# A linear-attention and channel-mix kernel rewritten: strided token tiles, k side first, normalised q features, token-major second matmul, loads on two queues, and a pipeline ordered by hand

## Chip, cores and metric

One core of one Trainium2 chip. The metric is the time of one execution on the device, in microseconds (us). All kernels named here were run on the chip; those of one experiment round share one chip and are timed beside runs of the kernel before. The changed kernel itself ran in a round of its own, so it and the experiments are compared across chips; the kernel before took a median of 303.0 to 304.1 us in all rounds. Every run has a state, fast or slow (slow: over 1.5% above the fastest run of the same kernel).

PE is the matmul engine, PEld its weight loads, DVE the vector engine, ACT the scalar engine, POOL the GpSimd engine, SP the engine that issues most DMA.

## The reference, cut to what matters

```python
# q, k, v: (4 batches, 4 heads, 1088 tokens, 32); S1, S2: (8, 32)
def phi(x):                                   # 64 features per token and head
    a = S1 x ; b = S2 x                       # 8 each
    return outer(a, b).reshape(64)
kv  = sum_s phi(k_s) v_s^T                    # 64 x 32 per batch and head
z   = sum_s phi(k_s)                          # 64
x   = (phi(q) kv) / (phi(q) . z + 1e-6)       # heads side by side: 128 wide
# then an RWKV channel mix on x (4 x 1088 x 128), d_ff = 1024
xk  = mu_k * x + (1 - mu_k) * x_prev          # x_prev: the token before
xr  = mu_r * x + (1 - mu_r) * x_prev
out = sigmoid(xr w_r) * (relu(xk w_k)**2 w_v)
```

The output is float32, (4, 1088, 128).

## The kernel before

Per batch: 9 tiles of 128 consecutive tokens (the last has 64). Only the parts that the argument touches are shown; cuts are marked.

```python
for b in range(B):
    # ... loads in tiles of 128 tokens: q_sb, k_sb, v_sb, all on the SP queue, runs of 128 bytes
    for t in range(n_tiles):                         # PE transposes of q and k, DVE copies
        nc.tensor.transpose(qtp[:, :m], q_sb[:m, t, :, :]..., ident[:m, :m])
        nc.vector.tensor_copy(qT_sb[:, t, :m], qtp[:, :m])
        # ... the same for k
    for t in range(n_tiles):                         # projections, float32
        nc.tensor.matmul(abk_ps[:], kT_sb[:, t, :], S12T_bd...)
        nc.tensor.matmul(abq_ps[:], qT_sb[:, t, :], S12T_bd...)
        # ... two DVE copies
    # ... k_p, q_p: outer products on DVE, 128 x 2304
    for h in range(H):
        for t in range(n_tiles):                     # L159, L160
            nc.tensor.transpose(qpT_ps[:, :m], q_p[:m, t, h, :], ident[:m, :m])
            nc.vector.tensor_copy(qpT_sb[:, t, :m], qpT_ps[:, :m])
        for t in range(n_tiles):                     # L164
            nc.tensor.matmul(kv_p[:], k_p[:tsz(t), t, h, :], v_sb[:tsz(t), t, h, :], ...)
        # ... kv_cat: 64 x 33, the 33rd column is z
        for t in range(n_tiles):                     # L175
            nc.tensor.matmul(num_ps[:, t, :], qpT_sb[:, t, :], kv_cat[:], ...)
        # ... divide by the 33rd column on DVE
    # ... transposes of x into xT
for b in range(B):                                   # channel mix
    # ... xk_bf, xr_bf on DVE
    while off < S:                                   # 512 tokens at a time
        for c in range(nchunks):                     # 8 chunks of d_ff
            nc.tensor.matmul(kpsum[:, :m], wk[:, c * P:(c + 1) * P], xk_bf[:, off:off + m])
            nc.scalar.activation(krelu[:, :m], kpsum[:, :m], RELU)
            nc.vector.tensor_mul(k2_bf[:, :m], krelu[:, :m], krelu[:, :m])
            nc.tensor.matmul(vvT_p[:, :m], wv[:, c, :], k2_bf[:, :m], ...)
        # ... gate, product, PE transposes back to token-major, stores
```

## Time and profile before

| | before |
|---|---|
| time, median of the first 3 runs | 302.0 us |
| PE, DVE, ACT busy | 259.5, 170.5, 50.3 us |
| attention / channel mix | 0 to about 225 us / 215 to 303 us |
| DMA packets | 62242, mostly under 512 bytes |

The first and second part of the page, before: busy time of each engine, and rows of 40 slices of the span, with the busy share in tenths, the clock granted to PE in tenths, and what DMA moved.

```profile
PE 259.5 (86%) x1212; PEld 184.6 (61%) x1212; DVE 170.5 (56%) x617; ACT 50.3 (17%) x110; POOL 0.7 (0%) x6
PE   0258799999979999998899999959979999698984
PEclk9999999999999999999555555555886559859798
GB/s 70 167 118 92 122 88 117 40 2 51 120 52 2 0 0 0 2 0 0 3 0 0 0 2 0 0 0 2 0 1 2 0 0 59 18 75 0 74 0 77
```

The chain of waits that ended last, before: by engine, and by line of the kernel.

```profile
PE 73%; DVE 12%; SPq 4%; DMA 4%; issue 3%; ACT 2%; DVEq 0%; ACTq 0%
PE num_ps L175 19%; PE qpT_ps L159 14%; PE kv_p L164 12%; PE vvT_p L214 5%; PE abk_ps L138 5%; PE abq_ps L139 5%; PE kpsum L209 5%; DVE k_p L150 3%; PE xtr_ps L187 3%; DVE k_bf L213 2%; PE qtp L125 2%; PE ktp L129 2%; ACT krelu L211 2%; DMA _t_96<-in_moe_w_r_dram 2%; PE otp L230 2%
```

### The profile page before, as it was taken

How to read it: one execution, taken by the hardware profiler on the slowest of the kernel's cores; microseconds unless marked ns; L12 is line 12 of the kernel's file. 1: busy time of each engine (PE TensorE's matmuls, PEld its weight loads, DVE VectorE, ACT ScalarE, POOL GpSimd, SP SyncE). 2: the span in 40 equal slices, each digit the busy share in tenths (PEclk: the TensorE clock that was granted, in tenths of full speed). 3: DMA queues.
4: the chain of work that ended last, by engine and by line, in shares of the span. 5: the costliest groups of instructions: out<-in, count | busy, mean ns of one | idle time of the engine just before them, and what ended most of it. 6: DMA issues, size and time to landing. Idle time of an engine off the chain costs nothing.

```text
span 303.0 us, 3582 instructions
## 1 busy us (share of the span) xinstructions
PE 259.5 (86%) x1212; PEld 184.6 (61%) x1212; DVE 170.5 (56%) x617; ACT 50.3 (17%) x110; POOL 0.7 (0%) x6
## 2 busy tenths in 40 slices
PE   0258799999979999998899999959979999698984
PEld 0127688667968866796677778948555654333432
DVE  3234733554374355448734445693646569877674
ACT  1000000000000000001000000000443146458682
POOL 0000000000000000000000000000000000000000
PEclk9999999999999999999555555555886559859798
DMA  3975757203730000000000000000000002020202
GB/s 70 167 118 92 122 88 117 40 2 51 120 52 2 0 0 0 2 0 0 3 0 0 0 2 0 0 0 2 0 1 2 0 0 59 18 75 0 74 0 77
DMA packets 62242, 10.27 MB, mean 34 GB/s; under 512 B 56592, under 2 KB 62096, under 8 KB 62224
## 3 DMA queue, kind: packets, MB, share of 16 engines
q1 hardware_dynamic: 62224, 10.04, 18.6%
q8 instruction: 10, 0.16, 0.2%
q14 instruction: 8, 0.07, 0.1%
HBM read 7.81 MB, written 2.23 MB: 33 GB/s over the span
## 4 chain that ended last, share of the span: by engine, by line
PE 73%; DVE 12%; SPq 4%; DMA 4%; issue 3%; ACT 2%; DVEq 0%; ACTq 0%
PE num_ps L175 19%; PE qpT_ps L159 14%; PE kv_p L164 12%; PE vvT_p L214 5%; PE abk_ps L138 5%; PE abq_ps L139 5%; PE kpsum L209 5%; DVE k_p L150 3%; PE xtr_ps L187 3%; DVE k_bf L213 2%; PE qtp L125 2%; PE ktp L129 2%; ACT krelu L211 2%; DMA _t_96<-in_moe_w_r_dram 2%; PE otp L230 2%
## 5 line engine op out<-in xcount | busy, mean ns | idle before, releaser
L211 ACT ACTIVATE krelu<-kpsum 128x512 bf16<-128x512 f32 (+1 forms) x96 | 43.0, 471 | 242.7 <-PE kpsum L209 149.6
L175 PE MATMUL num_ps<-kv_cat,qpT_sb 64*128 64x33 f32 x288 | 59.6, 378 | 0.0
L175 PEld LDWEIGHTS num_ps<-kv_cat,qpT_sb 64*128 64x128 f32 x288 | 57.6, 304 | 2.6 <-DVE qpT_sb L160 1.9
L159 PE MATMUL qpT_ps<-ident,q_p 128*64 128x128 f32 x144 | 51.9, 396 | 2.6 <-DVE qpT_sb L160 2.0
L160 DVE COPY qpT_sb<-qpT_ps 64x128 f32<-64x128 f32 x144 | 37.8, 274 | 22.4 <-PE qpT_ps L159 18.8
L164 PE MATMUL kv_p<-v_sb,k_p 128*64 128x33 f32 (+1 forms) x288 | 37.2, 297 | 8.2 <-DVE k_p L150 8.2
L164 PEld LDWEIGHTS kv_p<-v_sb,k_p 128*64 128x64 f32 (+1 forms) x288 | 33.5, 221 | 14.7 <-DVE k_p L150 9.8
L209 PE MATMUL kpsum<-xk_bf,wk 128*128 128x512 bf16 (+1 forms) x96 | 35.1, 386 | 5.3 <-ACT r_sb L220 2.0
L159 PEld LDWEIGHTS qpT_ps<-ident,q_p 128*64 128x64 f32 x144 | 18.8, 133 | 28.4 <-DVE qpT_sb L160 18.5
L214 PE MATMUL vvT_p<-k_bf,wv 128*128 128x512 bf16 (+1 forms) x96 | 32.6, 373 | 3.1 <-DVE k_bf L213 2.6
L213 DVE TENSOR_TENSOR k_bf<-krelu 128x512 bf16<-128x512 bf16 (+1 forms) x96 | 31.3, 339 | 6.7 <-ACT krelu L211 4.0
L125 PE MATMUL qtp<-ident,q_sb 128*128 128x128 f32 (+1 forms) x36 | 15.6, 434 | 17.1 <-DMA q_sb<-in_q_dram 16.0
L177 DVE MEMSET num_ps<- 64x33 f32 x16 | 1.4, 86 | 49.7 <-PE num_ps L175 49.7
L138 PE MATMUL abk_ps<-S12T_bd,kT_sb 128*128 128x64 f32 x72 | 22.5, 416 | 0.7 <-DVE abk_sb L140 0.7
L139 PE MATMUL abq_ps<-S12T_bd,qT_sb 128*128 128x64 f32 x72 | 22.5, 415 | 0.0
L214 PEld LDWEIGHTS <-wv 128*128 128x128 bf16 x96 | 10.9, 115 | 15.2 <-issue 11.9
L125 PEld LDWEIGHTS qtp<-ident,q_sb 128*128 128x128 f32 (+1 forms) x36 | 6.9, 192 | 21.3 <-issue 12.4
L138 PEld LDWEIGHTS abk_ps<-S12T_bd,kT_sb 128*128 128x128 f32 x72 | 18.0, 308 | 3.0 <-DVE abk_sb L140 2.0
L139 PEld LDWEIGHTS abq_ps<-S12T_bd,qT_sb 128*128 128x128 f32 x72 | 17.8, 305 | 1.0 <-DVE abq_sb L141 0.2
L209 PEld LDWEIGHTS <-wk 128*128 128x128 bf16 x96 | 11.0, 116 | 11.1 <-issue 8.5
L129 PE MATMUL ktp<-ident,k_sb 128*128 128x128 f32 (+1 forms) x36 | 15.5, 429 | 1.5 <-DMA k_sb<-in_k_dram 1.0
L127 DVE COPY qT_sb<-qtp 128x128 f32<-128x128 f32 (+1 forms) x36 | 9.8, 274 | 6.6 <-PE qtp L125 6.6
(53 smaller groups left out, 162.8 us busy)
## 6 DMA issues: line engine op xcount, KB each, us to landing
q_sb<-in_q_dram SPq DMA_DIRECT2D x32, 64.0 KB, 2.6
k_sb<-in_k_dram SPq DMA_DIRECT2D x32, 64.0 KB, 2.6
v_sb<-in_v_dram SPq DMA_DIRECT2D x32, 64.0 KB, 2.6
out_dram<-outT_s SPq DMA_DIRECT2D x4, 512.0 KB, 3.4
_t<-in_moe_w_k_dram SPq DMA_DIRECT2D x1, 512.0 KB, 3.3
_t_92<-in_moe_w_v_dram SPq DMA_DIRECT2D x1, 512.0 KB, 5.4
S12T_bd<-in_S_dram SPq DMA_DIRECT2D x8, 1.0 KB, 3.4
q_sb<-in_q_dram SPq DMA_DIRECT2D x4, 32.0 KB, 2.5
```

Source lines behind the costliest of these rows:

```text
L125: nc.tensor.transpose(qtp[:, :m], q_sb[:m, t, :, :].rearrange("p h d -> p (h d)"), ident[:m, :m])
L129: nc.tensor.transpose(ktp[:, :m], k_sb[:m, t, :, :].rearrange("p h d -> p (h d)"), ident[:m, :m])
L138: nc.tensor.matmul(abk_ps[:], kT_sb[:, t, :], S12T_bd[:].rearrange("p h x -> p (h x)"))
L139: nc.tensor.matmul(abq_ps[:], qT_sb[:, t, :], S12T_bd[:].rearrange("p h x -> p (h x)"))
L159: nc.tensor.transpose(qpT_ps[:, :m], q_p[:m, t, h, :], ident[:m, :m])
L160: nc.vector.tensor_copy(qpT_sb[:, t, :m], qpT_ps[:, :m])
L164: nc.tensor.matmul(kv_p[:], k_p[:tsz(t), t, h, :], v_sb[:tsz(t), t, h, :], start=(t == 0), stop=(t == n_tiles - 1))
L175: nc.tensor.matmul(num_ps[:, t, :], qpT_sb[:, t, :], kv_cat[:], start=st, stop=sp)
L209: nc.tensor.matmul(kpsum[:, :m], wk[:, c * P:(c + 1) * P], xk_bf[:, off:off + m])
L211: nc.scalar.activation(krelu[:, :m], kpsum[:, :m], RELU)
L213: nc.vector.tensor_mul(k2_bf[:, :m], krelu[:, :m], krelu[:, :m])
L214: nc.tensor.matmul(vvT_p[:, :m], wv[:, c, :], k2_bf[:, :m], start=(c == 0), stop=(c == nchunks - 1))
```

## The change

Its intent, as the code shows it: token s of a batch is written s = 17 p + t, so that one partition holds 17 consecutive tokens and a load moves runs of 2176 bytes; a tile holds 64 tokens of each of two batches. The sums over k are done first, for a half (two batches) at a time. The normaliser is turned into a projection (SW holds S2-weighted z), and q features are divided before the product with kv, so that x comes out feature-major, as the channel mix needs it. The second channel-mix matmul takes the squares as the stationary operand and gives tokens on the partitions, so that no output is transposed. Small matmuls are split over the array with tile positions. A loop over groups of 4 tiles runs the channel mix of group g beside the attention of groups g+2 and g+3.

The core of the diff, cut:

```diff
-        for t in range(n_tiles):
-            nc.sync.dma_start(q_sb[:m, t, :, :], q[b, :, s0:s0 + m, :].rearrange("h p d -> p h d"))
+    def load_tok(x, src, eng, b2):          # half on the SP queue, half on the GpSimd queue
+        eng.dma_start(tok[x][64 * b2:64 * b2 + 64],
+                      src[2 * int(x[1]) + b2].rearrange("h (s t) d -> s h t d", t=NT))
+    def load_hd(x, src):                    # head-major, for 32x32 transposes on DVE
+        nc.sync.dma_start(hd[x][:], src[...].rearrange("h (a c t) d -> (h a) c t d", a=32, c=2))
...
+    def transp_tok(dst, x, t0, t1):         # L154
+        for t in range(n):
+            for h in range(H):
+                nc.tensor.matmul(tp[D * h:D * h + D, t * P:t * P + P], tok[x][:, h, t0 + t, :], ident[:],
+                                 tile_position=(0, D * h))
+        nc.scalar.copy(dst[...], tp[:, :n * P])
+    def k_feat(half, gi):                   # L166
+        for t in range(n):
+            for c in range(4):
+                nc.tensor.matmul(abp[32 * c:32 * c + 32, t * 64:t * 64 + 64],
+                                 kT[half][:, t0 + t, 32 * c:32 * c + 32], SW[:, 0, :, :2, :],
+                                 tile_position=(0, 32 * c))
+        nc.scalar.copy(ab...) ; nc.vector.tensor_mul(kp...)
+    def k_acc(half, gi, ab, kp):            # L188, L195: 64x64 tiles
...
+    def q2(g):                              # normaliser and q features
+        nc.vector.tensor_mul(pw...) ; nc.vector.tensor_reduce(den...) ; nc.vector.reciprocal(den...)
+        nc.vector.tensor_mul(an...) ; nc.vector.tensor_mul(qp[g]...)
+    def q5(g):                              # x, feature-major; token shift and mix
+        nc.tensor.matmul(o[64 * pair:64 * pair + 64], kvbd[...], qpT[g]..., tile_position=(0, 64 * pair))
+        nc.scalar.activation(PP..., src, COPY, scale=omu_k[:])
+        nc.vector.scalar_tensor_tensor(XK..., src, mu_k[:], PP..., op0=MUL, op1=ADD)
+        nc.scalar.copy(XB..., src)
...
+    def mm2(g, cp):                         # L367
+        for c in range(2):
+            for t in range(n):
+                nc.tensor.matmul(ops[g][:, t * P:t * P + P], k2[:, c, t * P:t * P + P], wv[:, 2 * cp + c, :], ...)
...
+    for n in range(nn + 3):
+        g, cp = divmod(n, 4)
+        if n < nn: mm1(g, cp)
+        if cp == 0 and g + 3 < NQ: q1(g + 3)
+        if cp == 1 and g + 2 < NQ: q5(g + 2)
+        if cp == 1 and g + 3 < NQ: q2(g + 3)
+        if cp == 3 and g + 3 < NQ: Q4(g + 3)      # PE transposes of the q features
+        if cp == 2 and g < NQ: rr(g)
+        if n < nn: sq(g, cp)
+        if 2 <= n < nn + 2: mm2(*divmod(n - 2, 4))
+        if n >= 6 and cp == 2: fin(g - 1)
```

## The prediction

> **What bounds the kernel now.** The profile's first part: PE 259.5 us busy of 303.0 (86%), DVE 170.5, ACT 50.3. The chain of waits puts 73% of the span on PE: num_ps 19%, qpT_ps 14%, kv_p 12%, abk_ps and abq_ps 5% each. So attention is bound by narrow, costly float32 matmuls. Instruction starts show how: num_ps (128 stationary columns, 33 moving) starts every 213 ns, kv_p (64, 33) every 107 ns, unchanged where the granted clock is 0.5. That is the weight load, 1.67 ns per float32 column. The table of windows: attention fills 0 to 225 us, the channel mix mostly 215 to 303, with PE, DVE and ACT 60 to 85% busy. The first matmul starts at 11.9 us, behind weight loads on one queue.
>
> **What the change does.**
> 1. Token tiles of 2 KB runs on two queues, k first. First k features at 9 to 10 us (estimate: 3 us to landing of a 512 KB load[...]).
> 2. 288 num_ps (60 us) and 144 qpT_ps (52 us) disappear. Instead: 68 full transposes (107 ns at full clock as otp shows, 213 at half) and some 40 wide matmuls with kv stationary. The 72 transposes of x and out vanish.
> 3. Projections and transposes of k and q become 32-column tiles (408 matmuls), the k-v sum 340 matmuls of 64 columns. At the weight-load rate these cost 53 and 107 ns if tiles do not overlap. The Trainium skill ("TensorEngine Tiling (Array Packing)", Key Properties) says "Different tiles can execute LdWeights and Matmul in parallel" but changing mode drains; no run here shows either yet. I take 60 to 80 ns.
> 4. The normaliser moves onto q: with the 1024-wide product some 2.3 us of DVE per 4 tiles (from 2549 ns at 2304 wide).
> 5. Evictions are wide: RELU of 1024 about 1.02 us (596 ns at 512), square 0.68 (417 at 512). ACT takes half the copies.
> 6. The second matmul becomes 272 matmuls of 128 columns, each with its weight load (0.08 to 0.11 us).
>
> **On the critical path.** About 1,270 matmuls, as before (1212), but 85 to 100 ns each instead of 214. Head 10 us. K side with the first q groups: PE 54 us (27 sums, 22 projections and transposes, 5 other). Main loop per 4 tiles: PE 8 to 10 us, DVE 7.1, ACT 6.5 to 7, near balance: 9.5 us for six groups with q work, 6 for three without, 75 us. Tail 3, stalls 4. Sum 146 us; PE first, ACT and DVE close behind.
>
> **Prediction: 146 us**, eight in ten between 122 and 178. Faster by over 2%: 0.97; within 2%: 0.01; slower: 0.02.
>
> **What would show it.** PE near 120 us busy; kv starts near 80 ns apart, those of 32-column tiles near 60; first abp before 11 us; loop groups of 8.5 to 10 us; DVE near 83 us, ACT near 70 us busy; loads mostly over 2 KB a packet, done by about 45 us.
>
> **What would make it wrong.** Tiles of different column groups not overlapping, so that they cost their four moving passes (160 to 213 ns): up to 180 us. The clock granted at 0.5 over the k side or the loop: 512-wide matmuls then cost 427 ns and transposes 213, some 15 us more. Loads on the GpSimd queue arriving late and stalling the k side. On the other side, four-fold overlap brings the k side under 40 us and the whole to 125.

## More of the kernel before

The costliest PE groups, before: line, engine, operation, shapes, count, then busy time in all and mean ns of one, then idle time before them and what ended it.

```profile
L175 PE MATMUL num_ps<-kv_cat,qpT_sb 64*128 64x33 f32 x288 | 59.6, 378 | 0.0
L159 PE MATMUL qpT_ps<-ident,q_p 128*64 128x128 f32 x144 | 51.9, 396 | 2.6 <-DVE qpT_sb L160 2.0
L164 PE MATMUL kv_p<-v_sb,k_p 128*64 128x33 f32 (+1 forms) x288 | 37.2, 297 | 8.2 <-DVE k_p L150 8.2
```

PE bounds the attention part: it is 73% of the whole chain and is busy for 185 of the first 215 us. Two things in these lines are easy to misread, and I misread both when I predicted.

First, the program holds 144 num_ps matmuls (4 batches, 4 heads, 9 tiles), and the trace has 288 records: a float32 matmul leaves two records of weight load and two of matmul here, which I call its two passes. A transpose leaves one (144 qpT_ps in both).

Second, the clock row. The table of windows for num_ps alone, before: start and end of the window, its length, then busy time and count of each engine, PEclk, DMA share, GB/s.

```profile
58.00:61.98 3.98, 3.98 (x18) 3.84 (x18) 0.00 (x0) 1.00 0.00 0
215.42:217.40 1.98, 1.98 (x18) 1.87 (x17) 0.00 (x0) 1.00 0.00 0
239.72:243.70 3.98, 3.97 (x18) 3.84 (x18) 0.00 (x0) 0.50 0.00 0
```

The same 18 passes take 3.98 us at a recorded clock of 1.00, 1.98 us at 1.00, and 3.98 us at 0.50. The clock record of this trace starts with its first event, at 139.9 us, and what lies before is shown as full clock. By the durations PE ran at half clock there as well: transposes start 213 ns apart before 139.9 us, and 108 to 109 ns apart where the clock was really full. So almost all of the attention part before ran at half clock. The Trainium skill, page "TensorE: Matmul & The Clock Gate", section "What's actually happening", says that "the default state is throttled, and activity releases the throttle". The first half fits this trace: PE ran at half clock from the start. The second does not fit as it stands: from 30 to 139.9 us PE was busy for 104.6 of 109.9 us with narrow float32 matmuls and transposes, and their durations did not change. Which activity would have released the clock is not shown here.

## The result, and the profile after

The changed kernel takes 139.34 us median of 4 runs: two fast ones of 138.01 and 138.25, two slow ones of 140.44 and 140.92. The kernel before, in the same rounds: 302.98 us. The ratio is 0.456, with a 95% interval of 0.453 to 0.459. Ratios here are the mean time of one kernel's fast runs over that of the other's of the same rounds, so not quite the ratio of the medians that are quoted. The result is correct.

First and second part of the page, after; with the rows that were shown of before.

```profile
PE 98.8 (73%) x2054; PEld 75.1 (55%) x2065; DVE 78.3 (57%) x155; ACT 69.2 (51%) x117; POOL 8.4 (6%) x29
PE   3250958659997789496929949549949689698970
PEclk9999999986999999999999999986999999999998
GB/s 103 335 275 305 301 248 224 302 58 5 5 5 0 5 5 5 7 0 5 0 2 5 0 0 82 0 0 77 0 0 82 0 40 42 0 77 76 5 77 115
```

The chain of waits, after.

```profile
PE 50%; DVE 18%; ACT 13%; DMA 8%; issue 8%; SPq 1%; DVEq 0%; ACTq 0%
PE kv L188 9%; DMA tok_v_66<-in_v_dram 8%; PE tp L154 8%; PE qtp L277 7%; PE o L367 7%; PE h L347 6%; DVE qp L270 5%; DVE XK L333 4%; PE abwp L250 4%; PE abp L166 4%; PE kv L195 3%; PE xps L317 2%; ACT PP_150 L332 2%; ACT PP_149 L332 2%; DVE den L262 1%
```

PE work has more than halved, 259.5 to 98.8 us, in spite of more records (2054 for 1212). No single line is over 9% of the chain now; DVE, ACT, a load and "issue" (PE waits for nothing that the profile shows) are nearly half of it. Loads run at 220 to 335 GB/s after the first slice and end at 29.6 us; before they ran at 40 to 170 GB/s in the first 60 us and ended at 88 us.

PE groups of the attention part, after.

```profile
L188 PE MATMUL kv<-tok_v_66,kp 64*64 64x32 f32 x272 | 9.6, 269 | 8.1 <-issue 4.5
L166 PE MATMUL abp<-SW,kT_131 128*32 128x64 f32 x136 | 5.0, 314 | 3.5 <-DVE kT_131 L147 3.5
L154 PE MATMUL tp<-ident,tok_k_68 128*32 128x128 f32 x136 | 6.5, 345 | 0.2 <-ACT qpT L283 0.2
```

Tiles overlap. By the starts in the trace, tile records of one set of four stand about 7 ns apart, then up to 90 ns to the next set at full clock and up to 194 ns at half clock. Summed over the distances under 200 ns, 340 kv matmuls cost 14.5 us (43 ns each; about 34 at full clock and 61 at half), 136 abp 5.3 us (39 ns), 136 tp 8.3 us (61 ns). The Trainium skill ("TensorEngine Tiling (Array Packing)", Key Properties) says that different tiles can load and multiply in parallel; this trace agrees.

The windows view by stage, before (attention; both; channel mix) and after (head; first half of k while loads run; second half of k with the first q groups; the loop). Columns after the length: PE, PEld, DVE, ACT and POOL busy with counts, PEclk, DMA share, GB/s.

```profile
0.00:215.00 215.00, 185.38 (x874) 146.38 (x874) 111.59 (x415) 4.76 (x7) 0.70 (x6) 0.83 0.23 37
215.00:225.00 10.00, 7.48 (x51) 5.20 (x50) 5.58 (x23) 5.06 (x8) 0.00 (x0) 1.00 0.00 1
225.00:303.00 78.00, 66.67 (x291) 32.99 (x290) 53.34 (x180) 40.49 (x96) 0.00 (x0) 0.76 0.10 30
```

```profile
0.00:13.70 13.70, 3.80 (x69) 2.78 (x70) 7.74 (x24) 2.23 (x4) 6.46 (x15) 1.00 0.87 255
13.70:33.00 19.30, 14.79 (x418) 13.29 (x418) 2.88 (x3) 2.13 (x5) 1.98 (x14) 0.91 0.85 199
33.00:64.00 31.00, 25.41 (x892) 21.48 (x890) 15.51 (x28) 12.59 (x31) 0.00 (x0) 1.00 0.02 4
64.00:136.00 72.00, 54.81 (x686) 37.50 (x694) 52.18 (x100) 52.27 (x78) 0.00 (x0) 0.97 0.09 32
```

Attention alone took 215 us before. Now the k side with the first q groups takes 64 us, and the rest of attention hides in a loop of 72 us, not much shorter than the channel mix was alone. In that loop each engine is busy for 52 to 55 of 72 us: no engine is full.

The timeline of PE around two stretches in which it waits for nothing known, after: start, length, engine, line, operation, count, and in brackets the idle time before and what ended it.

```profile
18.51 0.40 PE L195 MATMUL kv<-ab 64*64 64x32 f32 x4
20.83 0.44 PE L188 MATMUL kv<-tok_v_66,kp 64*64 64x32 f32 x9 [1.92 <-issue]
...
25.63 0.40 PE L188 MATMUL kv<-tok_v_66,kp 64*64 64x32 f32 x4
28.63 0.36 PE L188 MATMUL kv<-tok_v_66,kp 64*64 64x32 f32 x10 [2.59 <-issue]
```

PE stops in the middle of a run of equal matmuls, whose data are there. Counting all PE instructions of the trace by their starts (its semaphore instructions too), the start after the gap is the one after instruction 449, then 705; two more gaps of 1.15 and 1.06 us stand after 1729 and 1985. All four are 193 plus a multiple of 256. From start to start the four gaps are 2.18, 2.88, 1.15 and 1.06 us, 7.3 us together (as idle time 6.2 us). The third part of the page lists queues; this one carries instructions:

```profile
q8 instruction: 16, 0.26, 0.8%
```

16 packets, 0.26 MB: 16 KB each. The Trainium skill ("Runtime: NRT & Kernel Launch", Instruction fetch mechanics) says that an engine's instructions are refilled in blocks of 16 KiB, 256 instructions, and that crossing a boundary is "mostly hidden". The trace agrees with the block size (4142 PE instructions and 16 packets; before 2507 and 10), and at 12 of the 16 boundaries PE goes on within 0.22 us. At the four gaps it disagrees about the cost.

The packets of this queue can also be read one by one in the trace's DMA records. At each of the four gaps one ends 1.4 to 1.5 us before PE starts again: at 19.46, 27.20, 41.67 and 45.40 us, for starts at 20.83, 28.62, 43.17 and 46.90. A packet starts soon after PE has crossed the boundary before: 1.2 and 1.1 us after it for the two late gaps, but 4.0 and 5.3 us after it for the two early ones, while loads run. So PE stalls where it uses up 256 instructions before the next block has come; from one crossing to the start after the next gap that took 6.5 and 7.8 us during the loads and 3.8 and 3.7 us after them.

The waits view, after, lines of the loop and its neighbours: engine, tile and line, what it waited for, us in total, times, longest.

```profile
PEld qtp L277 <- ACT r L381: 13.1, 6, 3.6
PE qtp L277 <- DVE qp L270: 11.8, 6, 3.2
DVE XK L333 <- ACT PP_150 L332: 6.5, 5, 2.2
ACT XB_148 L336 <- DVE XK L333: 3.6, 5, 0.8
ACT XB_147 L336 <- DVE XK L333: 3.6, 5, 0.8
```

PE waits six times, about 2 us each, for qp, the q features, before it can transpose them. The first line names ACT's r for the weight loads of the same transposes, but in all six groups r ends at least 0.3 us before qp, and the transposes start 0.1 to 0.2 us after qp's end: qp is the wait that ends last. In front of qp on DVE stands XK, the mix, which itself waited up to 2.2 us for ACT. ACT in turn makes its second copy of x, XB, only after the mix (last two lines).

The same shapes at two clocks, timeline of PE after: 32 transposes of the same kind, at half clock and after PE's clock rose at 32.9 us.

```profile
30.03 1.93 PE L154 MATMUL tp<-ident,tok_k_68 128*32 128x128 f32 x32
33.85 1.08 PE L154 MATMUL tp<-ident,tok_k_68 128*32 128x128 f32 x32
```

The clock record of this trace starts at 26.1 us. Before that it shows full clock, and the durations (kv 291 ns) say half. From 26.1 to 29.5 us the clock was full (kv 219 ns), then half until 32.9 us, then full but for 90.9 to 94.3 us and the last 0.9 us.

### The profile page after: what moved, and what is told of

It reads as the page before. It is cut to its first block, busy times and chain, and to the rows that moved or that the text cites. A ratio compares the mean times of both kernels' runs of the same rounds, so it can differ in the third digit from the quotient of the medians.

```text
span 136.2 us, 4574 instructions
## 1 busy us (share of the span) xinstructions
PE 98.8 (73%) x2054; PEld 75.1 (55%) x2065; DVE 78.3 (57%) x155; ACT 69.2 (51%) x117; POOL 8.4 (6%) x29
## 4 chain that ended last, share of the span: by engine, by line
PE 50%; DVE 18%; ACT 13%; DMA 8%; issue 8%; SPq 1%; DVEq 0%; ACTq 0%
PE kv L188 9%; DMA tok_v_66<-in_v_dram 8%; PE tp L154 8%; PE qtp L277 7%; PE o L367 7%; PE h L347 6%; DVE qp L270 5%; DVE XK L333 4%; PE abwp L250 4%; PE abp L166 4%; PE kv L195 3%; PE xps L317 2%; ACT PP_150 L332 2%; ACT PP_149 L332 2%; DVE den L262 1%
## 5 line engine op out<-in xcount | busy, mean ns | idle before, releaser
L174 DVE TENSOR_TENSOR kp<-ab 128x1024 f32<-128x1024 f32 (+1 forms) x10 | 10.6, 1064 | 23.3 <-ACT ab L170 23.1
L277 PE MATMUL qtp<-ident,qp 128*128 128x128 f32 x68 | 9.7, 284 | 13.9 <-DVE qp L270 11.8
L347 PE MATMUL h<-XK,wk 128*128 128x512 bf16 (+1 forms) x61 | 18.7, 374 | 0.5
L277 PEld LDWEIGHTS qtp<-ident,qp 128*128 128x128 f32 x68 | 7.4, 142 | 16.9 <-ACT r L381 13.1
L188 PE MATMUL kv<-tok_v_66,kp 64*64 64x32 f32 x272 | 9.6, 269 | 8.1 <-issue 4.5
L188 PEld LDWEIGHTS kv<-tok_v_66,kp 64*64 64x64 f32 x272 | 8.9, 185 | 9.7 <-issue 9.7
L195 PE MATMUL kv<-ab 64*64 64x32 f32 x136 | 11.3, 243 | 0.0
L270 DVE TENSOR_TENSOR qp<-an,abw 128x1024 f32<-128x1024 f32 (+1 forms) x9 | 10.5, 1165 | 0.3
L317 PE MATMUL xps<-qpT,kvbd 128*64 128x256 f32 (+3 forms) x80 | 9.4, 359 | 0.0
L195 PEld LDWEIGHTS kv<-ab 64*64 64x64 f32 x136 | 8.6, 163 | 0.0
L166 PE MATMUL abp<-SW,kT_131 128*32 128x64 f32 x136 | 5.0, 314 | 3.5 <-DVE kT_131 L147 3.5
L188 PE MATMUL kv<-tok_v_67,kp 64*64 64x32 f32 x272 | 6.5, 222 | 0.8 <-issue 0.8
L188 PEld LDWEIGHTS kv<-tok_v_67,kp 64*64 64x64 f32 x272 | 5.9, 133 | 1.8 <-issue 1.5
L347 PEld LDWEIGHTS <-wk 128*128 128x128 bf16 x72 | 5.7, 99 | 0.9 <-issue 0.7
```

The source lines that it names most:

```text
L166: nc.tensor.matmul(abp[32 * c:32 * c + 32, t * 64:t * 64 + 64], kT[half][:, t0 + t, 32 * c:32 * c + 32], SW[:, 0, :, :2, :], skip_group_ch ...
L174: nc.vector.tensor_mul(kp[:, :n], _ap(a_, list(a_.ap[1:]) + [[0, R]]), _ap(b_, list(b_.ap[1:3]) + [[0, R]] + [b_.ap[3]]))
L188: nc.tensor.matmul(kv[hp:hp + 64, b2, (h // 2) * D:(h // 2) * D + D], kp[rows, t - t0, h].rearrange("p i j -> p (i j)"), tok["v%d" % half] ...
L195: nc.tensor.matmul(kv[:64, b2, 64:64 + HR], ab[rows, t - t0].rearrange("p h x r -> p (h x r)"), ab[rows, t - t0, :, 1, :], start=False, st ...
L270: nc.vector.tensor_mul(qp[g][:, :n], _ap(a_, list(a_.ap[1:]) + [[0, R]]), _ap(b_, list(b_.ap[1:3]) + [[0, R]] + [b_.ap[3]]))
L277: nc.tensor.transpose(p[:, t * P:t * P + P], qp[g][:, t, 2 * pair:2 * pair + 2].rearrange("p h i j -> p (h i j)"), ident[:])
```

## The experiments

The theories, after the first look at the trace:

- A: column tiles make the k side cheap because they share weight loads; PE work decides the k side.
- B: the k side (14 to 64 us) is set by loads, by the supply of PE instructions and by waits from engine to engine, not by the amount of PE work.
- C: the loop (64 to 136 us) is a chain in program order, not one engine's busy time.

Twelve kernels were run. "Ratio" is to the kernel before; the changed kernel's is 0.456. "First wide matmul" is the first h (L347), the start of the loop. For e5 and e6 the record classes the comparison with the kernel before as "unclear" and does not say why; their ratios' intervals (0.474 to 0.485, 0.430 to 0.442) are far from 1.

| run | what | fast runs, us | ratio | first wide matmul to end, in the trace |
|---|---|---|---|---|
| changed kernel | | 138.0, 138.3 | 0.456 | 64.1 to 136.2 = 72.2 |
| e1 | k features untiled | 135.5 (3 slow: 137.7 to 138.9) | 0.456, but see e1 | 61.6 to 133.7 = 72.1 |
| e2 | no normaliser (wrong result) | 130.2, 132.1 | 0.432 | profile slow |
| e3 | DVE transposes for k and q | 132.0 to 132.6 | 0.436 | profile slow |
| e4 | few loads (wrong result) | 130.2 to 131.8 | 0.431 | 57.3 to 129.2 = 71.9 |
| e5 | PE transposes later in the loop | 144.7 to 146.3 | 0.480 | 63.6 to 143.3 = 79.7 |
| e6 | e5 and e9 | 131.1 to 132.8 | 0.436 | 64.4 to 129.8 = 65.4 |
| e7 | e3 and e1 | 134.0 (3 slow: 136.6 to 141.4) | none | profile slow |
| e8 | 64 dummy PE instructions | 138.5 (one run, state unknown) | none | 64.4 to 136.7 = 72.4 |
| e9 | order on DVE, and ACT's second copy earlier | 128.5 to 130.2 | 0.426 | 64.1 to 126.5 = 62.4 |
| e10 | dummies to raise the clock | 139.2 to 140.8 | 0.460 | profile slow |
| e11 | e3 and e6 | 126.1 to 127.0 | 0.417 | 59.0 to 124.3 = 65.3 |
| e12 | e3 and e9 | 122.1 to 123.7 | 0.407 | 58.2 to 120.3 = 62.1 |

### e1: k features without column tiles

```diff
-            for c in range(4):
-                nc.tensor.matmul(abp[32 * c:32 * c + 32, t * 64:t * 64 + 64],
-                                 kT[half][:, t0 + t, 32 * c:32 * c + 32], SW[:, 0, :, :2, :],
-                                 skip_group_check=True, tile_position=(0, 32 * c))
+            nc.tensor.matmul(abp[:, t * 64:t * 64 + 64], kT[half][:, t0 + t, :], SW[:, 0, :, :2, :],
+                             skip_group_check=True)
```

> The k features as one 128-column float32 matmul per token tile in place of four 32-column tiles. Theory A (tiles overlap four-fold and share the weight load: 136 tile matmuls took 5.3 us by their starts, 39 ns each): one untiled matmul is two passes of a 213 ns weight load, so 34 x (427 - 157) ns = 9 us more PE work; abp starts 213 ns apart, total 5 to 9 us longer, 143 to 148. Theory B (the k side is set by the supply of PE instructions and by waits, not by PE work): 408 PE instructions fewer, one or two of the stalls at every 256th instruction fewer, total within 3 us of the changed kernel or faster.

The group of abp in this run, to compare with L166 above (there two groups, 5.0 and 3.0 us).

```profile
L165 PE MATMUL abp<-SW,kT 128*128 128x64 f32 x68 | 12.8, 349 | 3.2 <-DVE kT L147 3.2
```

The tiles do save PE work: 12.8 us without them, 8.0 with. But the time did not rise: its one fast run is 135.5 us, against 138.0 and 138.3. (The ratio of 0.456 is not that of this run, which would be 0.447; it fits the mean of the three slow runs, 138.4 us.) The gaps at the 256-instruction boundaries are nearly gone (14 instruction packets for 16; at the boundaries of the k side no idle time over 0.6 us is left), and the first wide matmul starts at 61.6 us instead of 64.1. Theory A's 5 to 9 us longer did not come; B's forecast did. Three of the four runs were slow, so I claim "no slower", not a gain. Nor does the run show that PE work costs nothing there: 4.8 us of work came, gaps of 7.3 us fell to about 1 us, the clock stayed full from 26.9 us on, and the k side became only 2.5 us shorter. The parts are not separated.

### e8: are the gaps instruction fetch?

```diff
+    pad = psum.tile([P, 512], F32, name="pad", tag="aux")
+    for i in range(32):
+        nc.tensor.transpose(pad[:, :P], ident[:], ident[:])
     kT = [const.tile([FD, NT, P], ...
```

> 32 dummy transposes (64 PE instructions) early, where PE is idle; the result stays correct. If the gaps of 2.2 and 2.9 us come from the fetch of PE instructions in blocks of 256, they stay at instructions 449 and 705 counted from the start, that is 64 instructions earlier in the program's work, in the middle of other matmuls. If they come from waiting for data or from the work itself, they stay with the same matmuls and move to instructions 513 and 769. Time within 2 us of the changed kernel, or 2 us more from the dummies.

The timeline of PE, this run.

```profile
15.90 0.32 PE L191 MATMUL kv<-tok_v,kp 64*64 64x32 f32 x8
20.67 0.33 PE L191 MATMUL kv<-tok_v,kp 64*64 64x32 f32 x5 [4.45 <-issue]
...
24.22 1.29 PE L157 MATMUL tp<-ident,tok_k 128*32 128x128 f32 x20
28.46 0.44 PE L157 MATMUL tp<-ident,tok_k 128*32 128x128 f32 x4 [2.94 <-issue]
```

The gaps stand after instructions 449 and 705 again, though each instruction now carries work that came 64 instructions earlier: the second gap has moved out of kv into the middle of a run of transposes. So they belong to the count of instructions, not to the work or its data. And they end at the same time: PE came to the first boundary 2.6 us sooner (16.01 us for 18.65), since 64 of the count were dummies and its clock was full here (kv 219 ns), and started again at 20.67 us for 20.83; the second start is at 28.46 us for 28.62. PE waits there for something that comes at its own time. That this is the fetch is shown by the count, by e1 and by the packets, which here too end 1.4 to 1.5 us before these two starts.

### e4: few loads

k and v of the first half are loaded, the rest is read from those tiles.

```diff
-    tok = {x: const.tile(...) for x in ("v0", "v1", "k1", "q0")}
-    hd = {x: const.tile(...) for x in ("k00", "k01", "q10", "q11")}
+    tok = {x: const.tile(...) for x in ("v0",)} ; v1, k1, q0 are the same tile
+    hd = {x: const.tile(...) for x in ("k00", "k01")} ; q10, q11 are the same tiles
-    for x, src in (("v0", v), ("k1", k), ("q0", q), ("v1", v)):   # both queues
+    for x, src in (("v0", v),):
```

> Wrong result on purpose: only k of the first half and v of the first half are loaded, the other tiles are read from those (3.3 MB of loads less the weights instead of 7.8). Theory: loads hold the first kv matmul from about 10 to 13.7 us, and while they fill the DMA engines (to 29.6 us) they delay the fetch of PE instructions (gaps of 2.2 and 2.9 us at instructions 449 and 705). Without them kv starts at about 9 to 10 us and those two gaps fall to about 1 us or nothing: total 5 to 8 us shorter. Rival (k side bound by 54 us of PE work, as I predicted): under 3 us shorter, since PE would be busy anyway.

130.2 to 131.8 us, about 7 us less than the fast runs of the changed kernel. The first kv matmul starts at 12.9 us for 13.7, so the start itself gained under 1 us: v of the first half lands hardly sooner, since its load stands right behind k's in both kernels. The gaps after 449 and 705 are gone, and the packets that served them start 0.45 and 0.24 us after the crossing instead of 4.0 and 5.3; gaps of 0.7, 0.6 and 1.1 us at later boundaries stay. The first wide matmul starts 6.7 us earlier. So the loads cost about 7 us of the k side, 5 us of it in the two gaps of the delayed fetch; a part may be the clock, which rose at 21.9 us here. And half of my own theory (a start at 9 to 10 us) was wrong.

### e10: does the half clock before 33 us cost anything?

```diff
+    def warm_pe(n):                      # wsrc: a bf16 tile of 0.5
+        wp = psum.tile([P, 512], F32, name="wp", tag="aux")
+        for i in range(n):
+            nc.tensor.matmul(wp[:], wsrc[:, :P], wsrc[:], skip_group_check=True)
+    warm_pe(4)                           # before the first transposes
     ...
     B_(0, 1)
+    warm_pe(10)
     C_(0, 0)
```

> 14 dummy 512-wide bf16 matmuls in PE's idle stretches before 14 us; result correct. The durations say that PE runs at half clock until 33 us (32 tile transposes 1.93 us, later 1.08) although the clock record, which starts at 26 us, shows full clock before. Theory: dense matmuls raise the clock, tile matmuls with gaps do not; with the dummies the transposes at 23 us take about 1.1 us and the kv groups half as long. If half clock costs time on the path: 2 to 4 us shorter. If loads and the instruction fetch set this stretch anyway: within 1.5 us of the changed kernel, or up to 1 us longer.

The dummies did raise the clock for a while, from 11.2 to 18.1 us by the record: kv matmuls last 219 ns there, in the changed kernel 291. It fell again after that, so the transposes at 23 us did not become faster (1.87 us for 32), as I had expected. The fast runs are 139.2 to 140.8 us: no gain. The timeline of PE shows where the faster stretch went (the profile is of a slow run):

```profile
16.02 0.31 PE L197 MATMUL kv<-tok_v,kp 64*64 64x32 f32 x5
20.51 0.53 PE L197 MATMUL kv<-tok_v,kp 64*64 64x32 f32 x10 [4.18 <-issue]
```

PE came to the boundary sooner and waited longer, until 20.51 us (20.83 in the changed kernel). So half clock up to 18 us cost nothing here: the stretch ends when the block of instructions has come. What it costs from 18 to 33 us was not tested.

### e3 and e7: less PE work and fewer PE instructions on the k side

e3 loads k of the second half and q of the first head-major as well, and transposes them on DVE.

```diff
-    tok = {... ("v0", "v1", "k1", "q0")} ; hd = {... ("k00", "k01", "q10", "q11")}
+    tok = {... ("v0", "v1")} ; hd = {... ("k00", "k01", "k10", "k11", "q00", "q01", "q10", "q11")}
-    TK(0) ... TK(4), TQ(16, 17) ... TQ(12, 16)      # 272 PE tile matmuls, 10 ACT copies
+    transp_hd(kT[1], "k1", 0, 8) ; transp_hd(kT[1], "k1", 8, NT)      # at the places of TK(0), TK(1)
+    transp_hd(qT[0], "q0", 8, NT) ; transp_hd(qT[0], "q0", 0, 8)      # at the places of TQ(16, 17), TQ(0, 4)
```

> k and q of the other half also loaded head-major and transposed on DVE (16 more 32x32 transposes of 0.4 us, 6.4 us) in place of 272 float32 PE tile matmuls (8.3 us by their starts, 544 PE instructions) and ten ACT copies (5.3 us). Theory B (instruction supply and the chain PE, ACT, PE bound the k side): two stalls at every 256th instruction fewer and the PE work gone, k side 5 to 9 us shorter, total 130 to 134. Theory A' (PE work alone): 8.3 us less PE work of which half is on the path, 134 to 136. If DVE bounds the k side: no gain or slower.

132.0 to 132.6 us, inside B's forecast (130 to 134) and below that of A' (134 to 136). But the edit takes PE work, PE instructions and ACT copies away together, so this run alone does not tell them apart. In its trace, of a slow run, the two early gaps remain (2.7 and 2.9 us) and the two late ones are at most 0.4 us. In the traces of e11 and e12, which contain this edit, the first wide matmul starts at 58 to 59 us instead of 64. DVE had the room: 2.9 of 19.3 us busy between 13.7 and 33 us.

e7 adds the edit of e1 to that of e3.

> The DVE transposes of the third run and the untiled k features of the first run together: PE instructions 4142 to about 3190. Theory B (PE instruction supply): the gaps at 256-instruction boundaries before 30 us become fewer, since fewer instructions are used up there; total 129 to 132, at or below the third run's 132.5. Theory A (tile work): 5 us more PE work on the features, 134 to 137.

Inconclusive: 134.0 us in its one fast run, 136.6 to 141.4 in three slow ones. It is not better than e3, and the fast run is 1.4 us worse than e3's slowest fast one. That lies outside B's forecast (129 to 132) and at the edge of A's (134 to 137), so this run, as far as one run goes, speaks for PE work that counts. Whether its slow runs come from the edit or from chance stays open.

### e2: what the normaliser costs

```diff
-        nc.vector.tensor_mul(pw...) ; nc.vector.tensor_reduce(den...) ; nc.vector.reciprocal(den...) ; nc.vector.tensor_mul(an...)
-        a_ = an[:, :n]
+        a_ = x[:, :n, :, 1]              # wrong result
```

> Wrong result on purpose: the four small DVE operations of the normaliser on q are left out (9 x 1.1 us = 10 us of DVE busy time). If DVE bounds the loop: about 1.0 us less per group, total 8 to 10 us shorter. If the loop is a chain over three engines in which DVE's lateness only partly shows (the transposes of q features waited 11.8 us for qp): 3 to 7 us shorter. If ACT or PE bound it: under 2 us.

130.2 and 132.1 us: 7 us less, for 10 us of DVE work taken away. That is the top of the middle band: much of this DVE work is on the path, but not all of it shows. The profile is of a slow run, so where it showed is not read here.

### e5, e6, e9: the order in the loop

e5: PE's transposes of the q features (Q4) after the second matmuls of the step. e9: on DVE, the q features (q2) of group g+3 before the mix (q5) of group g+2, and ACT makes both its copies of x before the mix. ACT's own order stays; but its second copy no longer waits for the mix, and the mix waits for it. e6: both. The work is the same in all.

```diff
 e5:
-        if cp == 3 and g + 3 < NQ: Q4(g + 3)
         ...
         if 2 <= n < nn + 2: mm2(*divmod(n - 2, 4))
+        if cp == 3 and g + 3 < NQ: Q4(g + 3)
 e9:
-        if cp == 1 and g + 2 < NQ: q5(g + 2)
         if cp == 1 and g + 3 < NQ: q2(g + 3)
+        if cp == 1 and g + 2 < NQ: q5(g + 2)
     in q5:
+            nc.scalar.copy(XB..., src)
             nc.vector.scalar_tensor_tensor(XK..., src, mu_k[:], PP..., op0=MUL, op1=ADD)
-            nc.scalar.copy(XB..., src)
```

> In the fourth step of each loop group the transposes of the q features stand after the second matmuls of that step in PE's order, not before; same work. Theory C (the loop, 9.0 us a group with PE, DVE and ACT each 6.5 to 7.5 us busy, is a chain in program order: PE stands idle 1.6 to 3 us a group in front of these transposes, waiting for qp from DVE, while eight second matmuls that are ready stand behind them): 0.45 us of ready PE work fills each gap for six groups, total 2 to 4 us shorter. Rival (one engine's busy time bounds the loop): within 1 us.

A miss: 144.7 to 146.3 us, 7 us longer. The waits view of e5:

```profile
PEld L367 <- DVE k L357: 21.1, 12, 4.2
PE o L367 <- DVE k L357: 15.8, 9, 3.7
DVE XK L333 <- ACT PP L332: 12.5, 8, 2.8
```

The second matmuls that I took for ready were not. Their input is a square from DVE, and in DVE's order the squares stand behind qp. PE now waits for the squares first and does the transposes only after that; the loop is 7.5 us longer, about 1.3 us for each group with q work. Not all of it need be the order: in this loop the clock was at half for 15.1 us, in the changed kernel's for 4.4 us, and the two were not separated. What the wait in front of the transposes showed was DVE being late, not PE being in a bad order.

> As the run before, and DVE does the q features of group g+3 before the mix of group g+2, for which it waits for ACT; ACT makes both its copies before that mix. Same work. Theory C: DVE's wait in front of the mix (11.3 us in all by the waits view) is filled and qp is ready 1.5 us sooner, total 4 to 9 us shorter than the changed kernel. Rival (engine bound): within 1 us; slower if the later mix delays the first matmuls.

131.1 to 132.8 us, 6 us shorter than the changed kernel in spite of the move that costs.

> The other half of the sixth run alone: DVE does the q features of group g+3 before the mix of group g+2, ACT makes both copies before that mix, and the transposes stay where they were. The fifth run showed that moving the transposes alone costs 6 us, and both together gain 7. Theory C' (DVE's order sets the loop; the move of the transposes only makes the squares' users wait): DVE order alone gains 7 us or more, total 128 to 132. Rival (the two moves help only together): 134 to 139.

128.5 to 130.2 us, 9 us shorter (this alone was the forecast of 128 to 132), and the loop takes 62.4 us instead of 72.2. The waits view of e9; no line "PE qtp <- DVE qp" is left among its waits of over 1.7 us.

```profile
DVE XK L334 <- ACT XB L333: 3.6, 5, 1.3
PEld qtp L277 <- ACT r L381: 3.5, 4, 1.9
PEld L367 <- DVE k L357: 3.4, 8, 0.7
```

The same work, with its order changed on DVE and between ACT and DVE, is 10 us shorter in the loop. So no engine's busy time bounded it: the mix waited for ACT while q features that were ready stood behind it, and PE waited for those. Two things stay open. The edit makes two moves, q2 before q5 and ACT's second copy before the mix (7.2 us of ACT's waits in the changed kernel, nearly gone here), and no run tests them apart. And this loop was never at half clock, the changed kernel's for 4.4 us; as an estimate from that, the clock explains at most 2.2 of the 10 us, half of those 4.4.

### e11 and e12: do the gains add?

> The DVE transposes of the third run (132.5) with the loop order of the sixth (132.2). The first shortens the k side by about 4 to 6 us, the second the loop by 7, in different stretches, so if both theories hold the gains add: 125 to 128. If they were the same wait, 130 to 132.

> The DVE transposes of the third run with the DVE order of the ninth, the transposes of q features left where the changed kernel has them. The eleventh run (126.8) had the late transposes, which cost 3 us between the sixth (132.2) and the ninth (129.4). If that cost is in the loop alone: 123 to 125, k side as in the eleventh run (first h matmul near 59 us) and loop as in the ninth (62 us from first h to the end). If the ninth run's gain partly came from the k side: 125 to 127.

e11: 126.1 to 127.0 us. e12: 122.1 to 123.7 us, median 123.21, ratio 0.407 (0.404 to 0.409), correct. They add: the k side of e12 ends at 58.2 us as in e11, its loop takes 62.1 us as in e9. First part of the page of e12:

```profile
PE 90.9 (76%) x1782; PEld 69.4 (58%) x1793; DVE 83.1 (69%) x171; ACT 62.6 (52%) x107; POOL 9.3 (8%) x29
```

This version is faster than both kernels. Two gaps of 2.8 and 2.7 us after instructions 449 and 705 remain in it; loads still fill the DMA engines there.

## Why the prediction was right

It forecast 146 us, with 122 to 178; measured were 138.0 and 138.3 in fast runs. The reasons hold in part; the total is better than its terms.

| step of the prediction | predicted | measured | verdict |
|---|---|---|---|
| narrow float32 matmuls bound attention before, and vanish or are packed | PE 259.5 to about 120 us | 98.8 | right, the drop larger |
| "That is the weight load, 1.67 ns per float32 column", "unchanged where the granted clock is 0.5" | | 112 ns per 128-column pass at full clock, 213 at half | wrong |
| 32-column tiles and kv sums | 60 to 80 ns each | 43 (kv), 39 (abp), 61 (tp) | direction right, kv and abp too dear |
| second matmul, 128 columns | 80 to 110 ns | 55 ns (starts) | too dear |
| head | 10 us, first abp before 11 us | first abp 6.0 us, first kv matmul 13.7 us, held by v | abp right, kv late |
| "PE 54 us" on the k side | 54 of 54 us | PE busy 40 of the 50 us from 13.7 to 64 | the failed step |
| loop | 75 and 3 us, "PE first, ACT and DVE close behind" | 72.2 us, no engine over 55 busy | time right, reason wrong |
| DVE, ACT busy | 83, 70 | 78.3, 69.2 | right |
| loads | mostly over 2 KB, done by 45 us | done by 29.6 us | right, sooner |

The failed step is the size of the k side: "K side with the first q groups: PE 54 us". The k side did end at 64 us, where head plus 54 puts it, but by compensation, which is luck. The kv sums cost 14.5 us of the 27 that I took, and PE was busy for 40.5 us in all between 9.8 us, where its first abp end, and 64.1. The other 13.8 us are idle: 3.6 us for v, 6.2 us for PE instructions at four boundaries (e8, e4), the rest from engine to engine. I had listed late loads as a risk and had not thought of the instruction supply at all. Whether PE work counts there as well is not settled: e1 does not show it to be free, and e7 speaks for it.

The reading of the weight load failed in two ways that pull against each other. I compared num_ps at 0.5 with num_ps at a recorded 1.0 that was really 0.5, and so found no influence of the clock. And I counted one record as one matmul, when a float32 matmul is two. The cost per matmul at half clock by record (213 ns) is nearly that at full clock by matmul (two times 112), which is chance.

In the loop the durations of DVE and ACT (RELU of 1024 wide forecast at 1.02 us, about 1.04 measured; square 0.68, measured 0.69) were right. But "near balance: 9.5 us" took the fullest engine plus a margin. PE is busy for 6.4 to 7.5 us in a full group, not 8 to 10, and the groups still last 8.5 to 10.2 us: the time came out right by luck. e9 shows that the margin was waiting in order, of DVE for ACT above all: the same work runs in 62 us.

How much of the speedup is the clock, and how much the smaller work, stays open. Attention before ran at half clock nearly throughout, and the changed kernel from 33 us on nearly always at full clock. As an estimate from the two spacings, num_ps alone would have cost 288 x 112 ns = 32 us at full clock instead of the 60 us it had. No run here raised the clock of the kernel before.

## What to carry to other kernels

When no engine is full and the waits form a ring, look at the engine that waits while ready work stands behind the waiting instruction in its own order; moving that work forward (e9) gave more than any change of the work itself. Packing small matmuls into tiles multiplies PE instructions: count them, and look for gaps of PE without a cause that stand 256 instructions (or a multiple) apart, above all while loads run. Check a clock record against the durations of equal instructions before using it to tell what depends on the clock.

## What the Trainium skill lacked or had wrong

- "Runtime: NRT & Kernel Launch", Instruction fetch mechanics, says that a boundary of 16 KiB costs little, "mostly hidden". That holds for 12 of 16 boundaries here; four cost 1.06 to 2.88 us each, with tile matmuls about 7 ns apart. 408 instructions fewer (e1) left no idle time over 0.6 us at a boundary of the k side, and fewer loads (e4) removed the two long gaps. The section says nothing of loads that delay the fetch: its packet starts 4.0 and 5.3 us after the crossing during loads, 1.1 and 1.2 us later on.
- "TensorE: Matmul & The Clock Gate", LDWEIGHTS: the formula P / 1.2 names no clock. Here a float32 matmul pass with 128 stationary columns starts every 112 ns at full clock and every 213 ns at half.
- The same page does not say that a float32 matmul leaves two records with two weight loads; the program's 144 num_ps are 288 records. A float32 transpose is one record. (The page "FP8 and Floating Point Precision", TensorE Precision Notes, counts four passes for true float32; no run shows how many a record stands for.)
- The "activity releases the throttle" of "TensorE: Matmul & The Clock Gate" is not qualified for narrow float32 matmuls. Here 104.6 us of busy PE in 109.9 us, of narrow float32 matmuls and transposes, left the clock at half.
- "TensorEngine Tiling (Array Packing)" has a section "Instruction Overhead" on the time of one matmul, but not on the number of instructions that tiles add: 16 PE instructions per token tile for k features in place of 4. The saving of 4.8 us of PE work (12.8 to 8.0) bought no time here.
- No page that I read says that the granted-clock row shows full clock before the first record: before, 139.9 us of half clock appear as 1.00.
